# Every second one of the first sixteen weight pieces has its second float32r part subtracted by GpSimd instead of VectorE

## The chip, the cores and the metric

One core of one Trainium2 chip. The metric is the device time in microseconds of one execution; lower is better. The kernel before was timed three times: 563.71, 563.80 and 564.51 us, median 563.8.

## What is computed

Three stages in float32, 2 x 768 = 1536 tokens:

```python
# attention: 2 batches, 8 heads, 768 positions, head size 64
k_sum = k.reshape(B, H, 24, 32, D).max(axis=3)
v_sum = v.reshape(B, H, 24, 32, D).mean(axis=3)
scores_l = where(|i - j| < 16, q @ k.T / 8, -1e9)
scores_s = q @ k_sum.T / 8 + log(32)
a = softmax(concat(scores_l, scores_s));  x = a @ concat(v, v_sum)
# x as 1536 x 512
x = (sigmoid(x @ w_gate) * (x @ w_val)) @ w_out          # hidden size 1536
h = maximum(x @ w1, x @ w2, x @ w3)                      # hidden size 768
out = h @ w_out2
```

## The kernel before

**Two parts for each number.** TensorE multiplies in float32r. So that little of float32 is lost, each operand is held as two parts: a high part, which ScalarE writes by a copy into float32r (`hi`, L348), and the rest, which VectorE subtracts (`lo`, L351). A product is three matmuls: high by high, high by rest, rest by high.

**Weights.** They lie in HBM as 64-bit words (the bits of float64), 48 pieces of 128 x 512. `convert` takes them in the order of use; the pieces of the first block (w_gate, w_val, w_out) are converted a second time for the second batch, so there are 96 conversions. For each one: SP issues a load of 512 KB into `raw` (L398; three buffers), VectorE makes float32 bits of it by three integer instructions into `c` (L405, L410, L414; two buffers), ScalarE writes the high part into `w`, and VectorE the rest (L351, called in `split` at L429). A weight piece may be used when both are there (`wready`); `c` is free when both have read it. The first sixteen, counted from 0, are g0, v0, g1, v1, g2, v2, g3, v3 (gate and value, 128 hidden columns each), o0 to o3 (rows of w_out), g4, v4, g5, v5.

**Attention.** Sixteen units (batch, head pair, half of the sequence), numbered 0 to 15; units 0 to 3 are the first half of batch 0. Per unit: scores (PE L592), their masked maximum (VectorE L599, two times three instructions on `s` in PSUM), exponentials with their sums (ScalarE L605), a reciprocal (L610, L611), the normalisation (VectorE L614 up to unit 5, ScalarE L619 after that), transposes (PE L624), copies (ScalarE L627), the product with the values (PE L634), and the two parts of x (ScalarE L348, VectorE L351 `x<-s,x`). The block maxima of the keys are L516 (`ks`); for batch 1 they are copied into the window's keys (L574, `kw`). The block means of the values are matmuls for batch 0 (L522); for batch 1 GpSimd first adds them up (L527, three additions of 96 partitions with 512, 256 and 128 elements), then one matmul (L532). These additions and the constants are all that GpSimd does.

**First block.** For each half of a batch (`a`) and each group of four hidden pieces: `make_A` computes gate and value (PE L713, 12 matmuls each), ScalarE the sigmoid (L727), VectorE the product (L732, `t`), ScalarE and VectorE the two parts of the hidden piece (L348, L351 `h<-t,h`). Then `make_B` computes the four output blocks of the down projection (PE L747), each of four parts, one per hidden piece, of three matmuls; a block needs all four pieces of `h` and all four `o`. "The first down projection" is that of the first half of batch 0, hidden pieces 0 to 3.

**After that** come the second block (L837, by seven products in place of eight) and the last projection (L944).

**What sets the order.** Every step is a `Task` with an engine, a duration in us that is written in by hand (`add("DVE", 0.602, ...)`), a due time and its dependences. `Plan.order` (L115) goes through them like a clock: each engine takes, of the tasks that can start first, the one that is due first. The result is the order in which the instructions are issued; each engine, SP's DMA queue among them, then executes its own list in that order. A duration or an engine that is changed for one task moves the tasks behind it, on every engine. The planner's durations don't know of one engine slowing another.

Of the kernel before, what the change touches and what calls it, by code (L numbers as in the profile page):

```python
# [9 lines left out]
F32 = mybir.dt.float32  # L10
# [4 lines left out]
ALU = mybir.AluOpType  # L15
# [20 lines left out]
FREE_M = 2  # L36
BY_ACT = 6
BY_DMA = 8
JOINT = 4
SWITCH = 6.0  # L40
SLACK = {"PE": 0.05, "DVE": 0.12, "ACT": 0.1, "POOL": 0.0, "SP": 0.0}
# [31 lines left out]
class Plan:  # L73
# [11 lines left out]
    def add(self, eng, dur, due, fn, deps=(), new=(), uses=(), after=(), tab=None):  # L85
        t = Task(eng, dur, due, fn, [d for d in deps if d], list(new), list(uses), [d for d in after if d], tab)
        self.tasks.append(t)
        return t
# [114 lines left out]
def kernel(  # L203
# [15 lines left out]
    nc = tc.nc  # L219
# [67 lines left out]
    add = plan.add  # L287
# [59 lines left out]
    def hi(dst, src):  # L347
        nc.scalar.activation(out=dst, in_=src, func=ACTF.Copy)  # L348

    def lo(dst, src, h):  # L350
        nc.vector.tensor_tensor(out=dst, in0=src, in1=h.bitcast(F32), op=ALU.subtract)  # L351
# [26 lines left out]
    def first_use(b, nm, f):  # L378
        if nm == "o":
            return due["B", b, (f // GF, 0), 0] + 0.49 * (f % GF)  # L380
        if nm == "l":
            return due["D", 0, 0, 0] + 0.65 * f
        return due[nm, b, f, 0]

    wt, wready = {}, {}

    def convert():
        prev = {}
        n = 0

        def to_float(ck, t):

            nonlocal n
            r = Buf(rp, [128, 2 * 512], I32, "raw", 3)
            c = Buf(cp, [128, 512], I32, "c", 2)

            def load(r=r, ck=ck):
                nc.sync.dma_start(out=r.t, in_=wts[row[ck[1:]]])  # L398

            def half(r, i):  # L400
                return r.t.rearrange("p (f two) -> p f two", two=2)[:, :, i]


            def c1(r=r, c=c):
                nc.vector.tensor_scalar(  # L405
                    out=c.t, in0=half(r, 1), scalar1=5, scalar2=2,
                    op0=ALU.logical_shift_left, op1=ALU.logical_shift_right)

            def c2(r=r, c=c):
                nc.vector.scalar_tensor_tensor(  # L410
                    out=c.t, in0=half(r, 1), scalar=-0x40000000, in1=c.t, op0=ALU.bitwise_and, op1=ALU.bitwise_or)

            def c3(r=r, c=c):
                nc.vector.scalar_tensor_tensor(  # L414
                    out=c.t, in0=half(r, 0), scalar=29, in1=c.t, op0=ALU.logical_shift_right, op1=ALU.bitwise_or)

            n += 1
            l = add("SP", 1.456, t - WLOAD - WLOAD0 * (n <= 10), load, new=[r], after=[prev.get("l")])
            k1 = add("DVE", 0.335, t - 2.7, c1, [l], [c], [r], [prev.get("1")])
            k2 = add("DVE", 0.602, t - 2.3, c2, [k1], [], [c, r])  # L420
            k3 = add("DVE", 0.602, t - 1.6, c3, [k2], [], [c, r])
            prev.update({"l": l, "1": k1})
            return c, k3

        def split(src, view, t, dep, n=512):

            w = Buf(wp, [128, 2, 512], F32R, "w", NW)
            k4 = add("ACT", 0.52 if n == 512 else 0.31, t - 1.0, lambda: hi(w.t[:, 0, 0:n], view()), dep, [w], [src], [prev.get("4")])
            k5 = add("DVE", 0.602 if n == 512 else 0.38, t - 0.5, lambda: lo(w.t[:, 1, 0:n], view(), w.t[:, 0, 0:n]), [k4], [], [src, w])  # L429
            prev["4"] = k4  # L430
            return w, k5

        for ck in chunks:
            t = first_use(*ck) - WREADY
            c, k = to_float(ck, t)
            wt[ck], wready[ck] = split(c, lambda c=c: c.t.bitcast(F32), t, [k])
        for nm, f, b in groups:
            if b == 0:
                blocks(nm, f, to_float, split, prev)
        for ck in last:  # L440
            t = first_use(*ck) - WREADY
            c, k = to_float(ck, t)
            wt[ck], wready[ck] = split(c, lambda c=c: c.t.bitcast(F32), t, [k])
# [106 lines left out]
    def make_unit(u, i):  # L550
# [26 lines left out]
        def vfill(dma):  # L577
            o = vt.t[96:CW].rearrange("p t par h d -> p (t par) (h d)")
            src = vs.t[96:CW, None, :].to_broadcast([NB, 2 * TPU, 2 * D])
            if dma:  # L580
                nc.scalar.dma_start(out=o, in_=src)
            else:
                nc.scalar.activation(out=o, in_=src, func=ACTF.Copy)
# [72 lines left out]
        for h in range(2):  # L656
            m1 = add("DVE", 0.62, T - 9 + h, lambda h=h: maxi(h), [s1, built], [], [ps[h], e[h], nm])
            E.append(add("ACT", 1.14, T - 8 + h, lambda h=h: expo(h), [m1], [], [e[h], nm, sm], tab="E"))
            attention.extend([m1, E[h]])
        joint = i >= JOINT  # L660
        for h in range(2):
# [10 lines left out]
            attention.extend([i1, n1, t1, u1])  # L672
        dma = i >= BY_DMA
        g1 = add("ACT", 0.12 if dma else 0.83, T - 5, lambda: vfill(dma), [kv], [], [vt, vs], [lv])
# [309 lines left out]
    with tc.manual_schedule():  # L984
        idle = const.tile([128, 384], BF16, name="idle")
        nc.vector.memset(idle, 0.0)
        for t in plan.order():
            for b in t.new:
                b.take()
            if t.idle:  # L990
# [3 lines left out]
                n = min(o.shape[1], 384)  # L994
# [62 lines left out]
```

## Time and profile before

| | us |
|---|---|
| median of three runs | 563.8 |
| the profiled execution | 564.15 |
| its span in the trace | 562.2 |
| TensorE busy in the span | 545.4 |
| VectorE busy | 430.6 |
| ScalarE busy | 286.9 |
| GpSimd busy | 16.0 |

The span is the time from the first to the last event that the profile has; some 2 us of the execution lie around it. "Busy" counts the time in which an instruction of the engine runs; matmuls overlap one another, so TensorE can be called busy and yet be behind its pace. In the views in order of time a line stands for one or several instructions of a kind: start, length, engine, line, operation, output and inputs, the count, and in brackets the idle time before it with what ended it. In the chain of waits the second number is the part of the instruction that lies on the chain.

### The profile page before, as it was taken

Reading aid. Unit: us, or ns where it says so; the run is one execution under the profiler, and the core shown is the slowest. Engines: PE = TensorE matmul, PEld = TensorE weight load, DVE = VectorE, ACT = ScalarE, POOL = GpSimd, SP = SyncE. Lnnn points to the kernel's source line nnn. Section 1 sums busy time; section 2 is a strip of 40 time slices with the busy share of each in tenths; the row PEclk is TensorE's granted clock in tenths of the full one; section 3 lists DMA queues with packets and bytes.
Section 4 is the critical chain, followed back from the end, with each engine's and each line's share of the span. In section 5 each row is a group of like instructions: output and inputs, shape, how many; then the busy total and the mean of one; then the engine's idle time right before and its main releaser. Section 6 shows DMA issues by size and latency. Waiting matters only on the chain.

```text
span 562.2 us, 10234 instructions
## 1 busy us (share of the span) xinstructions
PE 545.4 (97%) x3924; PEld 522.4 (93%) x3924; DVE 430.6 (77%) x987; ACT 286.9 (51%) x663; POOL 16.0 (3%) x30
## 2 busy tenths in 40 slices
PE   7799899999999999999999999999999999999997
PEld 7688799998999999999999999999999999997886
DVE  5899949894697598949996996899999997885000
ACT  3789776582765656966441432435344333453111
POOL 2002211000000000000000000000000000000000
PEclk8999999999999999999999999999999999999999
DMA  8999654563265453520652553130322222000111
GB/s 275 311 284 303 192 174 152 154 216 97 85 194 184 145 154 107 170 75 1 188 186 77 157 182 113 53 98 23 105 90 85 77 74 86 28 1 37 57 72 60
DMA packets 24672, 71.96 MB, mean 128 GB/s; under 512 B 3120, under 2 KB 6576, under 8 KB 24624
## 3 DMA queue, kind: packets, MB, share of 16 engines
q1 hardware_dynamic: 21504, 67.58, 38.3%
q10 hardware_dynamic: 3120, 3.74, 1.9%
q8 instruction: 31, 0.51, 0.4%
q14 instruction: 17, 0.14, 0.1%
HBM read 67.57 MB, written 3.15 MB: 126 GB/s over the span
## 4 chain that ended last, share of the span: by engine, by line
PE 79%; DVE 10%; ACT 4%; DMA 4%; issue 1%; SPq 1%; ACTq 0%; DVEq 0%
PE m L713 28%; PE m L747 16%; PE s L837 11%; PE m L837 11%; PE m L944 9%; DVE c L414 2%; DVE c L410 2%; PE s L634 2%; DMA kn<-in_kn_dram 1%; DMA v<-in_vw_dram 1%; DMA vn<-in_vn_dram 1%; DVE w L351 1%; PE s L624 1%; DVE e L599 1%; DVE c L405 1%
## 5 line engine op out<-in xcount | busy, mean ns | idle before, releaser
L713 PE MATMUL m<-x,w 128*128 128x384 f32 x1152 | 211.0, 338 | 0.5 <-ACT t L727 0.3
L713 PEld LDWEIGHTS m<-x,w 128*128 128x128 f32 x1152 | 198.7, 188 | 2.5 <-issue 0.6
L747 PE MATMUL m<-h,w 128*128 128x384 f32 x576 | 107.5, 338 | 0.8 <-DVE h L351 0.7
L747 PEld LDWEIGHTS m<-h,w 128*128 128x128 f32 x576 | 99.2, 188 | 2.4 <-DVE h L351 1.7
L348 ACT ACTIVATE w<-c 128x512 fp32r<-128x512 f32 x96 | 58.1, 610 | 70.4 <-DVE c L414 46.1
L351 DVE TENSOR_TENSOR w<-c,w 128x512 fp32r<-128x512 f32 x96 | 64.4, 671 | 12.6 <-ACT w L348 12.4
L414 DVE SCALAR_TENSOR_TENSOR c<-raw,c 128x512 int32<-128x512 int32 x96 | 66.2, 692 | 0.6
L410 DVE SCALAR_TENSOR_TENSOR c<-raw,c 128x512 int32<-128x512 int32 x96 | 65.7, 686 | 0.6
L837 PE MATMUL m<-x,w 128*128 128x384 f32 x294 | 56.3, 335 | 1.2 <-ACT t L852 1.2
L837 PE MATMUL s<-f,w 128*128 128x384 f32 x294 | 56.0, 334 | 0.0
L837 PEld LDWEIGHTS m<-x,w 128*128 128x128 f32 x294 | 51.3, 188 | 1.6 <-ACT t L852 1.5
L837 PEld LDWEIGHTS s<-f,w 128*128 128x128 f32 x294 | 51.4, 188 | 0.0
L405 DVE TENSOR_SCALAR c<-raw 128x512 int32<-128x512 int32 x96 | 41.0, 430 | 5.1 <-DMA raw<-in_wts_dram 4.1
L727 ACT ACTIVATE t<-m 128x384 f32<-128x384 f32 x48 | 23.4, 491 | 34.9 <-PE m L713 34.6
L732 DVE TENSOR_TENSOR t<-m,t 128x384 f32<-128x384 f32 x48 | 26.6, 554 | 15.0 <-PE m L713 10.5
L348 ACT ACTIVATE h<-t 128x384 fp32r<-128x384 f32 x48 | 25.0, 522 | 25.5 <-DVE t L732 23.6
L605 ACT ACTIVATE e<-e,nm 128x120 f32<-128x120 f32 x96 | 36.6, 383 | 0.2
L351 DVE TENSOR_TENSOR h<-t,h 128x384 fp32r<-128x384 f32 x48 | 27.9, 582 | 5.4 <-ACT h L348 5.4
L954 ACT ACTIVATE c<-m 128x512 f32<-128x512 f32 (+1 forms) x13 | 7.3, 565 | 40.0 <-PE m L944 36.1
L852 ACT ACTIVATE t<-s 128x384 f32<-128x384 f32 x27 | 13.3, 491 | 24.4 <-PE s L837 24.4
L944 PE MATMUL m<-w,x 128*128 128x512 f32 (+1 forms) x126 | 24.9, 359 | 0.0
L944 PE MATMUL m<-w,f 128*128 128x512 f32 x108 | 24.7, 389 | 0.0
(108 smaller groups left out, 588.6 us busy)
## 6 DMA issues: line engine op xcount, KB each, us to landing
raw<-in_wts_dram SPq DMA_DIRECT2D x96, 512.0 KB, 3.6
kn<-in_kn_dram SPq DMA_DIRECT2D x8, 400.0 KB, 7.5
q<-in_qt_dram SPq DMA_DIRECT2D x16, 192.0 KB, 6.4
v<-in_vw_dram SPq DMA_DIRECT2D x16, 192.0 KB, 5.1
kw<-in_kw_dram SPq DMA_DIRECT2D x8, 360.0 KB, 4.1
out_dram<-c ACTq DMA_DIRECT2D x11, 256.0 KB, 2.0
vn<-in_vn_dram SPq DMA_DIRECT2D x8, 256.0 KB, 6.2
v<-in_vw_dram SPq DMA_DIRECT2D x16, 96.0 KB, 4.3
```

The costliest lines, as they stand in the source:

```text
L348: nc.scalar.activation(out=dst, in_=src, func=ACTF.Copy)
L351: nc.vector.tensor_tensor(out=dst, in0=src, in1=h.bitcast(F32), op=ALU.subtract)
L405: nc.vector.tensor_scalar(out=c.t, in0=half(r, 1), scalar1=5, scalar2=2, op0=ALU.logical_shift_left, op1=ALU.logical_shift_right)
L410: nc.vector.scalar_tensor_tensor(out=c.t, in0=half(r, 1), scalar=-0x40000000, in1=c.t, op0=ALU.bitwise_and, op1=ALU.bitwise_or)
L414: nc.vector.scalar_tensor_tensor(out=c.t, in0=half(r, 0), scalar=29, in1=c.t, op0=ALU.logical_shift_right, op1=ALU.bitwise_or)
L605: nc.scalar.activation(out=e[h].t[:, t], in_=e[h].t[:, t], func=ACTF.Exp, scale=-1.0, bias=nm.t[:, h, t:t + 1], accum_out=sm.t[:, h, t:t + 1])
L713: nc.tensor.matmul(ps.t, lhsT=w.t.rearrange("p s (k f) -> p s k f", k=KC)[:, wh, kc], rhs=src[kc // 2].t[:, xh, kc % 2], start=(kc == 0 an ...
L727: k1 = after("t", add("ACT", 0.371, end, lambda: nc.scalar.activation(out=s.t, in_=ps.t, func=ACTF.Sigmoid), [l], [s], [ps], tab="S"))
L732: k2 = after("t", add("DVE", 0.469, end, lambda: nc.vector.tensor_tensor(out=t.t, in0=ps2.t, in1=s.t, op=ALU.mult), [l2, k1], [t], [ps2, s]))
L747: nc.tensor.matmul(ps.t, lhsT=w.t.rearrange("p s (k f) -> p s k f", k=KC)[:, wh, dm], rhs=h.t[:, xh], start=(i == 0 and j == 0), stop=(i = ...
L837: nc.tensor.matmul(ps.t, lhsT=w.t[:, wh, c:c + 128], rhs=x.t[:, xh, kc], start=new and n == 0, stop=n == 5, skip_group_check=True)
L944: nc.tensor.matmul(ps.t[:, c0:c1], lhsT=h.t[:, xh, e, c:c + 128], rhs=w.t[:, wh, c0:c1], start=(f == 0 and i == 0), stop=(f == NF2 - 1 and ...
```

## The change

In `split`, the second part of a piece is subtracted by GpSimd where fewer than sixteen pieces have been made and their number is odd: v0, v1, v2, v3, o1, o3, v4, v5 (pieces 1, 3, 5, 7, 9, 11, 13, 15). The planner takes 1.4 us for it on GpSimd where it took 0.602 us on VectorE. For the other pieces the same subtraction is written out. The lines behind it move by one to five: L351 for weights becomes L433, L348 L349, L405 L406, L410 L411, L414 L415, L351 for x and h L352, L516 L521, L574 L579, L592 L597, L599 L604, L610 L615, L611 L616, L624 L629, L634 L639, L713 L718, L732 L737, L747 L752.

```diff
--- before.py
+++ after.py
@@ -36,6 +36,7 @@
 FREE_M = 2
 BY_ACT = 6
 BY_DMA = 8
+BY_POOL = 16
 JOINT = 4
 SWITCH = 6.0
 SLACK = {"PE": 0.05, "DVE": 0.12, "ACT": 0.1, "POOL": 0.0, "SP": 0.0}
@@ -425,8 +426,12 @@
         def split(src, view, t, dep, n=512):
 
             w = Buf(wp, [128, 2, 512], F32R, "w", NW)
+            pool = len(wready) < BY_POOL and len(wready) % 2 == 1
+            by = (nc.gpsimd if pool else nc.vector).tensor_tensor
+            eng = ("POOL", 1.4) if pool else ("DVE", 0.602 if n == 512 else 0.38)
             k4 = add("ACT", 0.52 if n == 512 else 0.31, t - 1.0, lambda: hi(w.t[:, 0, 0:n], view()), dep, [w], [src], [prev.get("4")])
-            k5 = add("DVE", 0.602 if n == 512 else 0.38, t - 0.5, lambda: lo(w.t[:, 1, 0:n], view(), w.t[:, 0, 0:n]), [k4], [], [src, w])
+            k5 = add(*eng, t - 0.5, lambda: by(out=w.t[:, 1, 0:n], in0=view(), in1=w.t[:, 0, 0:n].bitcast(F32), op=ALU.subtract),
+                     [k4], [], [src, w])
             prev["4"] = k4
             return w, k5
```

Since durations and engines enter the planner, the order changes on all engines up to about a quarter of the program.

On GpSimd, behind the constants, stood the additions of the block means of batch 1 (`vn`, `vr`):

```order
L282 MEMSET masks 64x16
L283 MEMSET masks 64x16
L527 TENSOR_TENSOR vn<-vn 96x2x256
L527 TENSOR_TENSOR vn<-vn 96x2x128
L527 TENSOR_TENSOR vr<-vn 96x128
L527 TENSOR_TENSOR vn<-vn 96x2x256
L527 TENSOR_TENSOR vn<-vn 96x2x128
L527 TENSOR_TENSOR vr<-vn 96x128
```

Now:

```order
L284 MEMSET masks 64x16
L433 TENSOR_TENSOR w<-c,w 128x512 x4
L532 TENSOR_TENSOR vn<-vn 96x2x256
L532 TENSOR_TENSOR vn<-vn 96x2x128
L532 TENSOR_TENSOR vr<-vn 96x128
L433 TENSOR_TENSOR w<-c,w 128x512 x2
L532 TENSOR_TENSOR vn<-vn 96x2x256
L532 TENSOR_TENSOR vn<-vn 96x2x128
L532 TENSOR_TENSOR vr<-vn 96x128
L433 TENSOR_TENSOR w<-c,w 128x512 x2
```

The pieces come in between; each `w` row is a subtraction of one weight piece, and the additions of a later head pair stand ahead of the later pieces.

On VectorE, the stretch between the product of the fourth hidden piece (`t`, L732) and the rest of the third (`h`, L351) before:

```order
L732 TENSOR_TENSOR t<-m,t 128x384
L516 TENSOR_REDUCE ks<-kn 128x24
L405 TENSOR_SCALAR c<-raw 128x512
L574 COPY kw<-ks 128x3x24 x2
L410 SCALAR_TENSOR_TENSOR c<-raw,c 128x512
L351 TENSOR_TENSOR h<-t,h 128x384
```

Now, from the rest of the third hidden piece (`h`) to the product of the fourth (`t`) and one row further (`c` and `raw` are the weight conversion, `sm` the reciprocal of unit 6, `x` that of unit 5):

```order
L352 TENSOR_TENSOR h<-t,h 128x384
L411 SCALAR_TENSOR_TENSOR c<-raw,c 128x512
L615 TENSOR_SCALAR sm<-sm 128x6
L616 RECIPROCAL sm<-sm 128x6
L352 TENSOR_TENSOR x<-s,x 128x384
L415 SCALAR_TENSOR_TENSOR c<-raw,c 128x512
L406 TENSOR_SCALAR c<-raw 128x512
L579 COPY kw<-ks 128x3x24 x2
L737 TENSOR_TENSOR t<-m,t 128x384
L411 SCALAR_TENSOR_TENSOR c<-raw,c 128x512
```

The rest of the third piece stands ahead of the product of the fourth, where it stood behind it, and two more steps of a weight conversion and a reciprocal are between the two.

On TensorE, at the start of the first down projection (`m<-h,w`; three matmuls are one part) with the scores and transposes of units 7 and 6, before:

```order
L713 MATMUL m<-x,w 128x384 x9
L747 MATMUL m<-h,w 128x384 x6
L634 MATMUL s<-at,v 64x64 x12
L592 MATMUL s<-kn,q 64x96 x12
L592 MATMUL s<-ks,q 64x24 x12
L747 MATMUL m<-h,w 128x384 x18
L624 MATMUL s<-ident,e_918 120x128 x3
L747 MATMUL m<-h,w 128x384 x3
L624 MATMUL s<-ident,e_919 120x128 x3
L747 MATMUL m<-h,w 128x384 x9
L634 MATMUL s<-at,v 64x64 x12
```

Now:

```order
L718 MATMUL m<-x,w 128x384 x12
L752 MATMUL m<-h,w 128x384 x6
L597 MATMUL s<-kn,q 64x96 x12
L597 MATMUL s<-ks,q 64x24 x12
L752 MATMUL m<-h,w 128x384 x3
L629 MATMUL s<-ident,e_931 120x128 x3
L752 MATMUL m<-h,w 128x384 x3
L629 MATMUL s<-ident,e_932 120x128 x3
L752 MATMUL m<-h,w 128x384 x15
L639 MATMUL s<-at,v 64x64 x12
L752 MATMUL m<-h,w 128x384 x21
```

Before, 24 matmuls (eight parts) of the projection stood ahead of the first transposes of unit 6; now 9 (three parts) do.

## Rows read from the trace of the kernel before

**Rows 1.** The page, busy times of the engines (share of the span, instructions).

```profile
PE 545.4 (97%) x3924; PEld 522.4 (93%) x3924; DVE 430.6 (77%) x987; ACT 286.9 (51%) x663; POOL 16.0 (3%) x30
```

**Rows 2.** Busy time by stretch: TensorE, weight loads, VectorE, ScalarE, GpSimd, clock, DMA share, GB/s.

```profile
30.00:70.00 40.00, 36.72 (x489) 32.60 (x481) 39.75 (x129) 35.29 (x99) 5.48 (x6) 1.00 0.83 262
```

**Rows 3.** The chain of waits, 24 to 110 us: start, us on the chain, what.

```profile
29.40 0.56 DVE x L351
...
32.27 0.20 DVE e L599
...
33.28 0.60 DVE w L351
...
40.66 0.60 DVE c L410
41.27 0.34 DVE c L405
...
63.73 0.86 DVE ks L516
...
64.92 0.23 DVE kw L574 x2
...
65.74 0.48 DVE h L351
```

**Rows 4.** TensorE in order of time, 59 to 69 us: start, us, what, idle before.

```profile
59.45 0.52 PE L624 MATMUL s<-ident,e 128*120 128x128 f32 x3 [1.58 <-DVE e L614]
...
66.27 2.18 PE L747 MATMUL m<-h,w 128*128 128x384 f32 x11 [0.45 <-DVE h L351]
```

**Rows 5.** Groups on GpSimd, 76 to 79 us: busy us, mean ns, idle before.

```profile
L527 POOL TENSOR_TENSOR vn<-vn 96x512 f32<-96x512 f32 x1 | 1.3, 1278 | 5.8 <-DMA vn<-in_vn_dram 5.8
```

**Rows 6.** VectorE and then GpSimd in order of time, near GpSimd's bursts.

```profile
30.92 0.42 DVE L405 TENSOR_SCALAR c<-raw 128x512 int32<-128x512 int32 x1
...
43.92 0.69 DVE L351 TENSOR_TENSOR w<-c,w 128x512 fp32r<-128x512 f32 x1
...
48.02 0.55 DVE L351 TENSOR_TENSOR h<-t,h 128x384 fp32r<-128x384 f32 x1
...
53.41 1.56 DVE L351 TENSOR_TENSOR w<-c,w 128x512 fp32r<-128x512 f32 x1
55.01 0.84 DVE L405 TENSOR_SCALAR c<-raw 128x512 int32<-128x512 int32 x1
...
67.47 1.45 DVE L351 TENSOR_TENSOR h<-t,h 128x384 fp32r<-128x384 f32 x1
68.85 0.27 DVE L599 CUSTOM_DVE_ANT_0 e<-s,masks 128x120 f32<-128x120 f32 x1
...
97.68 1.48 DVE L414 SCALAR_TENSOR_TENSOR c<-raw,c 128x512 int32<-128x512 int32 x1
...
53.14 2.42 POOL L527 TENSOR_TENSOR vn<-vn 96x512 f32<-96x512 f32 x2 [48.11 <-PE s L592]
...
67.23 2.29 POOL L527 TENSOR_TENSOR vn<-vn 96x512 f32<-96x512 f32 x2 [11.06 <-DMA vn<-in_vn_dram]
...
97.33 2.43 POOL L527 TENSOR_TENSOR vn<-vn 96x512 f32<-96x512 f32 x2
```

**Rows 7.** The chain of waits of the whole span: start, us, what.

```profile
251.91 16.64 PE m L713 x96
```

**Rows 8.** TensorE in order of time, 98 to 129 us.

```profile
98.48 1.47 PE L747 MATMUL m<-h,w 128*128 128x384 f32 x7
100.23 0.62 PE L747 MATMUL m<-h,w 128*128 128x384 f32 x2 [0.29 <-DVE h L351]
...
100.94 2.33 PE L747 MATMUL m<-h,w 128*128 128x384 f32 x12
103.42 0.92 PE L634 MATMUL s<-at,v 120*64 120x64 f32 x24
...
128.29 0.92 PE L634 MATMUL s<-at,v 120*64 120x64 f32 x24 [1.04 <-issue]
```

## The prediction

> **What bounds the kernel now.** The page first [rows 1]: TensorE is busy for 545.4 of 562.2 us, VectorE (DVE) for 430.6, GpSimd (POOL) for 16.0. By that share VectorE is not the bound, and relieving it would be worth nothing. A share is an average, though, so the next view is the table of stretches [rows 2]: between 30 and 70 us VectorE is busy for 39.75 of 40 us and GpSimd for 5.48, and TensorE has the holes. The chain of waits agrees [rows 3]: from the second L351 into x at 29.40 to the third L351 into h, which ends at 66.22, it runs through VectorE nearly without a break, and the pieces between are the weight conversion (L405, L410, L414, L351), the attention and the hidden parts. At 66.27 TensorE takes the chain over. In the list of TensorE's work [rows 4] one sees the holes: 1.58 us at 59.45 for a normalised e, 0.45 at 66.27 for the third h. So the change can act on the time in one place: how early VectorE gets through its work up to about 68.9 us, where the fourth h is done and TensorE's first down projection (L747) can go on.
>
> **What is taken off VectorE.** One subtraction into w takes 0.60 us of VectorE's time [rows 3] (the L351 w at 33.28). Eight leave it, so 8 x 0.60 = 4.8 us by about 95 us. What matters is the part ahead of the fourth h. By the order, between the second x and the fourth h VectorE had nine subtractions into w and now has four: 5 x 0.60 = 3.0 us less. The planner fills that room with work that stood behind the fourth h: one more conversion (L405, L410, L414), one more key maximum (L516), two copies into kw (L574), three score maxima (L599). From the chain [rows 3] that is 0.34 + 0.60 + 0.60 (L414 as L410) + 0.86 + 0.23 + 3 x 0.20 = 3.23 us. So VectorE has **0.23 us more to do before the fourth h**, not less. The third h has gained (in the order it now stands ahead of the fourth t), yet all four hidden pieces are needed before the first bank of the down projection is complete, and TensorE executes in order.
>
> **What it costs on GpSimd.** The page shows no 128x512 subtraction there. The nearest row is the L527 addition of 96x512, the same 512 elements on each partition: 1278 ns [rows 5]. I take 1.28 us. As a duration this is covered: the pieces are wanted later than they are ready. The first bank needs o1 and o3 (pieces 9 and 11) at about 60 and 69 us. On GpSimd they stand behind the first L527 burst, whose two larger additions ended at 53.14 + 2.42 = 55.56 [rows 6] and a short third one some 0.6 later; 56.2 + 1.28 = 57.5. If that cover goes, the third rival below gives the price.
>
> **What it costs VectorE.** This is the unknown price. Before the change GpSimd ran next to a busy VectorE only in a few bursts, and they can be read one by one [rows 6]. When L527 starts at 53.14, the L351 into w takes 1.56 us in place of its 0.69 (+0.87). At 67.23 the L351 into h takes 1.45 in place of 0.55 (+0.90). At 97.33 an L414, as large as the L351 of 0.69, takes 1.48 (+0.79). The smaller L527 behind the first stretches an L405 from 0.42 to 0.84. The L599s that run beside the second burst keep their 0.27. So an instruction of VectorE that reads two tensors from SBUF, or an L405, waits almost until GpSimd's addition is done; one that reads PSUM does not. Bounds of the stall for one moved subtraction: nothing (it meets only L599s, or an idle VectorE, as before the x at 29.40), and 0.90 us. Between the second x and the fourth h the sensitive kinds make some 60% of VectorE's time, they come in runs, and all three large bursts with work beside them met one. I take 0.65 us, three quarters of the middle of those three. That is more than the 0.60 that moving the subtraction saves: **on balance the move gives VectorE nothing**.
>
> The rows give the stall to the kinds that read two tensors. The Trainium skill, in "Advanced Engine Details and Errata" (VectorE Performance Modes), says that the second port shared with GpSimd makes GpSimd and two-port-mode Vector instructions block each other; by that alone only the L405s would suffer. "GPSIMD Engine Reference" (Key points) of the Trainium skill adds instructions with two SBUF inputs. The trace agrees with the second. By the first the stall would be nearly nothing, which is the first rival's sum.
>
> **The sum.** Pieces 3, 5, 7, 9 and 11 run on GpSimd between the second x and the fourth h (piece 1 falls where VectorE waits anyway before 29.40). The fourth h started at 67.47. With the change: 67.47 + 0.23 + 5 x 0.65 = 70.95. Its own length is 0.55, or 1.45 if the second L527 burst meets it again as in [rows 6]; half of that 0.90 gives an end near 71.95, against 68.92. TensorE goes on 3.0 us later. By then it has done one L747 part less than before (three matmuls at 0.173, the pace of 16.64 us for 96 [rows 7]: 0.52) and three transposes more (about 0.3), which leaves 0.2 more to do: **+3.2 us**. From there TensorE is the bound, with the same work as before, and a delay stays unless it swallows a later wait. The list shows two [rows 8]. Seven L747s at 98.48 take 1.75 us to the next, 1.21 at pace, and twelve at 100.94 take 2.48 to the L634 at 103.42, 2.08 at pace: they wait for an h, 0.94 in all. A TensorE that comes 3 us later finds that h ready, because VectorE then has 4.8 us less of its own work; I take back 0.8. The wait of 1.04 at 128.29 is named issue, no engine's lateness: nothing back. Sum +3.2 - 0.8 = **+2.4 us**.
>
> Edits that I cost at nothing: two more table loads on ScalarE at about 60 us (1.28 us each). They stand ahead of the scaling of unit 6, which waits for VectorE's reciprocal at least as long by the same sum; were they exposed, up to 1.3 us. Weight loads move one or two places ahead on SP's queue, past q and v loads; the DMA engines are at 0.83 of their time there and move 262 GB/s [rows 2], so a load that is passed lands later by about 512 KB at that rate, 2 us, and I see no TensorE wait for q or v in that stretch that would grow by it.
>
> The profiled execution took 564.15 us, 0.35 above the median of 563.8. 564.15 + 2.4 = 566.55; against the median **566.2 us**.
>
> **Rivals.**
> First, the other side: the stalls don't come about, because the pieces fall beside L599, L732 and L516 or because only L405 is hit. Then the fourth h ends at 67.47 + 0.23 + 0.55 = 68.25, 0.65 earlier than before, less 0.2 for the changed order, and the 0.8 at 99 us comes back too: 563.8 - 1.25 = **562.5 us**. For it: more than half of VectorE's instructions by number are the short L599s, which keep their length. Against: three bursts of three. It decides when the mean stall of a piece is under about 0.05 us. By the narrower note of the Trainium skill, above, it would go this way.
> Second, half the stall, 0.33 us a piece: 5 x 0.33 + 0.23 + 0.2 - 0.8, plus the half chance of the second burst, less what h already lost to it (0.45 - 0.90): +0.8, **564.6 us**. Within 0.2%, which is 1.1 us and about what a measurement of this kernel can tell from no change.
> Third, worse: GpSimd's queue. Pieces 9 and 11 stand behind an L527 that waits for a vn load. If that load lands 4 us later than before (53.1), piece 9 is ready at 61.5 or later and the first L747s wait for it, and all five stalls come in full: 5 x 0.9 + 0.23 + 0.45 + 0.2 = 5.4, without the 0.8 back: **569.1 us**. Against it: the place of that load on SP's queue is unchanged.
>
> **Chances.** Forecast (slower by more than 1.1 us, near 566.2) 0.54; third rival 0.08; second 0.22; first 0.16. So slower 0.62, same 0.22, faster 0.16. The range, 562.4 to 568.8, takes in the first rival and, at the top, the forecast with all five stalls at 0.90 (+1.25), the second burst met in full (+0.45) and 0.8 not given back: 568.7. What is left out is the third rival and a part of the first. For the forecast alone it is 565.0 to 568.7.
>
> **What would show it.** L351 into w (now L433 on GpSimd) at 1.2 to 1.4 us; some L410, L414 or L351 at about 1.5 us beside nearly every one of them; VectorE still above 39 of 40 us from 30 to 70; the fourth h ending at 71 to 73 us and TensorE waiting for an h there; after 130 us the same list of TensorE's work, 2 to 3 us later. I am wrong if VectorE's instructions keep their lengths beside GpSimd's, if the fourth h comes before 69 us, or if TensorE's wait at that place is for something else.

## The result and the profile after

The changed kernel takes **568.03 us** (median of four runs, 567.61 to 568.19), the kernel before in the same comparison 563.95: a ratio of 1.0071 with a 95% interval of 1.0053 to 1.0089. Run again beside other kernels later it gave 568.27, ratio 1.0087 (1.0060 to 1.0115). So it is slower by some 4 us, as forecast in sign, and by more than the 2.4 us of the sum. The profiled execution took 567.93 us with a span of 566.0.

The page's busy line answers to [rows 1], then the table of stretches to [rows 2]:

```profile
PE 546.3 (97%) x3924; PEld 524.7 (93%) x3924; DVE 427.3 (75%) x979; ACT 290.9 (51%) x665; POOL 26.4 (5%) x38
```

```profile
30.00:70.00 40.00, 35.78 (x438) 32.23 (x435) 38.12 (x127) 35.86 (x94) 11.12 (x10) 0.91 0.78 251
```

Three things are new between 30 and 70 us: GpSimd is busy for 11.12 us (5.48 before), VectorE is no longer without a gap (38.12 of 40, 39.75 before), and the granted clock is 0.91 where it was 1.00. Next the group of the eight moved subtractions, on GpSimd:

```profile
L433 POOL TENSOR_TENSOR w<-c,w 128x512 fp32r<-128x512 f32 x8 | 10.7, 1333 | 65.9 <-ACT w L349 65.9
```

VectorE in order of time, the instructions between the second x and the fourth h that took longer than their kind, or waited, and the fourth h itself:

```profile
33.53 0.17 DVE L615 TENSOR_SCALAR sm<-sm 128x3 f32<-128x3 f32 x1 [0.52 <-ACT e L610]
...
37.59 1.42 DVE L406 TENSOR_SCALAR c<-raw 128x512 int32<-128x512 int32 x1
...
47.99 0.79 DVE L352 TENSOR_TENSOR h<-t,h 128x384 fp32r<-128x384 f32 x1
...
51.91 0.56 DVE L737 TENSOR_TENSOR t<-m,t 128x384 f32<-128x384 f32 x1 [0.98 <-PE m L718]
52.38 0.94 DVE L415 SCALAR_TENSOR_TENSOR c<-raw,c 128x512 int32<-128x512 int32 x1
53.25 0.70 DVE L615 TENSOR_SCALAR sm<-sm 128x6 f32<-128x6 f32 x1
...
54.52 1.55 DVE L619 TENSOR_TENSOR e<-e,sm 128x360 f32<-128x360 f32 x1
...
64.40 0.78 DVE L352 TENSOR_TENSOR h<-t,h 128x384 fp32r<-128x384 f32 x1
...
70.66 0.94 DVE L352 TENSOR_TENSOR h<-t,h 128x384 fp32r<-128x384 f32 x1
```

GpSimd in order of time, over the same stretch and up to 97 us:

```profile
30.54 1.47 POOL L433 TENSOR_TENSOR w<-c,w 128x512 fp32r<-128x512 f32 x1 [17.40 <-ACT w L349]
37.44 1.29 POOL L433 TENSOR_TENSOR w<-c,w 128x512 fp32r<-128x512 f32 x1 [5.43 <-ACT w L349]
46.93 1.43 POOL L433 TENSOR_TENSOR w<-c,w 128x512 fp32r<-128x512 f32 x1 [8.21 <-ACT w L349]
51.48 2.44 POOL L532 TENSOR_TENSOR vn<-vn 96x512 f32<-96x512 f32 x2 [3.12 <-DMA vn<-in_vn_dram]
54.00 0.46 POOL L532 TENSOR_TENSOR vr<-vn 96x128 f32<-96x128 f32 x1
54.41 1.27 POOL L433 TENSOR_TENSOR w<-c,w 128x512 fp32r<-128x512 f32 x1
63.42 1.35 POOL L433 TENSOR_TENSOR w<-c,w 128x512 fp32r<-128x512 f32 x1 [7.74 <-ACT w L349]
...
93.53 1.29 POOL L433 TENSOR_TENSOR w<-c,w 128x512 fp32r<-128x512 f32 x1 [4.89 <-ACT w L349]
94.78 2.16 POOL L532 TENSOR_TENSOR vn<-vn 96x512 f32<-96x512 f32 x2
```

Put side by side, the two lists give the price of each piece. Piece 3 (30.54) ran beside score maxima and stretched nothing; piece 5 (37.44) made an L406 1.42 for 0.42; piece 7 (46.93) an h 0.79 for 0.55; piece 9 (54.41) the normalised e of unit 5 1.55 for 0.52; piece 11 (63.42) an h 0.78 for 0.55. That is 0 + 1.00 + 0.24 + 1.03 + 0.23 = 2.50 us.

The size follows from the place. Piece 5 ends at 37.44 + 1.29 = 38.73, and the L406 that started at 37.59 ends 0.28 us later, at 39.01; the e ends 0.39 behind piece 9, the two h 0.42 and 0.41 behind pieces 7 and 11. Each is 0.13 or 0.14 short of the instruction's own length. So a stalled instruction behaves as if it began 0.13 us before GpSimd's ends, and its stall is what is left of GpSimd's instruction at its start, less 0.13. An instruction that started first keeps its length: beside the start of piece 7 an L406 (46.79) took 0.42. There it is GpSimd that waits: piece 7 took 1.43 and piece 3, which started 0.31 us before the end of an L411, 1.47, where piece 5 took 1.29.

TensorE in order of time shows what it became there, and at about 99 us and 131 us the places of [rows 8]:

```profile
36.83 0.54 PE L629 MATMUL s<-ident,e 128*120 128x128 f32 x3 [0.76 <-DVE x L352]
...
43.16 0.62 PE L718 MATMUL m<-x,w 128*128 128x384 f32 x2 [0.66 <-DVE x L352]
...
56.22 0.52 PE L629 MATMUL s<-ident,e 128*120 128x128 f32 x3 [1.16 <-DVE e L619]
...
57.72 0.77 PE L629 MATMUL s<-ident,e 128*120 128x128 f32 x3 [0.51 <-DVE e L619]
...
99.56 0.62 PE L752 MATMUL m<-h,w 128*128 128x384 f32 x2 [1.13 <-DVE h L352]
...
131.48 0.92 PE L639 MATMUL s<-at,v 120*64 120x64 f32 x24 [0.86 <-issue]
```

The start differs from execution to execution (the second x comes at 28.77 to 32.30 us), so the table that the experiments are read with counts from the start of the second x on VectorE (29.40 before, 28.79 after), in us, one profiled execution each. The third column is the block of 51 gate and value matmuls at about 80 us, the fourth the L634 that is the last row of [rows 8] (L639 after).

| kernel | order, who subtracts | fourth h ends | 51 matmuls start | last row |
|---|---|---|---|---|
| before | old, VectorE | 39.52 | 50.32 | 98.89 |
| after | new, GpSimd | 42.81 | 53.62 | 102.69 |
| after, again | new, GpSimd | 43.90 | 54.66 | 103.55 |
| order only | new, VectorE | 43.33 | 53.81 | 102.27 |
| fill, new order | new, GpSimd fills | 41.14 | 51.75 | 99.49 |
| old order | old, GpSimd | 39.37 | 51.26 | 101.58 |
| fill, old order | old, GpSimd fills | 38.58 | 50.12 | 98.61 |
| idle subtractions | old, VectorE | 40.18 | 52.49 | 101.15 |
| after, with empty matmuls | new, GpSimd | 43.32 | 53.78 | 102.61 |
| before, with empty matmuls | old, VectorE | 39.17 | 49.84 | 97.80 |
| twelve pieces | new, GpSimd | 43.44 | 54.29 | 102.29 |
| all but piece 9 | old, GpSimd | 38.17 | 50.00 | 100.25 |
| all but 9, fill | old, GpSimd fills | 38.25 | 49.03 | 97.11 |
| pieces 1, 3, 11 | old, GpSimd | 37.74 | 49.30 | 97.63 |

### The profile page after: what moved, and what is told of

It is laid out like the page before. It is cut to its first block, busy times and chain, and to the rows that moved or that the text cites. A ratio compares the mean times of both kernels' runs of the same rounds, so it can differ in the third digit from the quotient of the medians.

```text
span 566.0 us, 10244 instructions
## 1 busy us (share of the span) xinstructions
PE 546.3 (97%) x3924; PEld 524.7 (93%) x3924; DVE 427.3 (75%) x979; ACT 290.9 (51%) x665; POOL 26.4 (5%) x38
## 4 chain that ended last, share of the span: by engine, by line
PE 83%; DVE 6%; ACT 4%; DMA 4%; issue 1%; SPq 1%; ACTq 0%; DVEq 0%
PE m L718 31%; PE m L752 17%; PE s L842 11%; PE m L842 11%; PE m L949 9%; PE s L639 2%; DMA q<-in_qt_dram 1%; PE s L629 1%; DVE c L415 1%; DMA raw<-in_wts_dram 1%; DMA vn<-in_vn_dram 1%; DVE c L411 1%; ACT e L610 1%; DVE c L406 1%; PE s L597 1%
## 5 line engine op out<-in xcount | busy, mean ns | idle before, releaser
L718 PE MATMUL m<-x,w 128*128 128x384 f32 x1152 | 213.1, 340 | 1.9 <-ACT x L349 1.0
L718 PEld LDWEIGHTS m<-x,w 128*128 128x128 f32 x1152 | 201.4, 190 | 3.8 <-ACT x L349 1.1
L752 PE MATMUL m<-h,w 128*128 128x384 f32 x576 | 107.0, 338 | 1.1 <-DVE h L352 1.1
L752 PEld LDWEIGHTS m<-h,w 128*128 128x128 f32 x576 | 99.3, 188 | 2.1 <-DVE h L352 1.5
L349 ACT ACTIVATE w<-c 128x512 fp32r<-128x512 f32 x96 | 58.1, 611 | 66.3 <-DVE c L415 42.9
L433 DVE TENSOR_TENSOR w<-c,w 128x512 fp32r<-128x512 f32 x88 | 57.8, 658 | 13.6 <-ACT w L349 13.3
L411 DVE SCALAR_TENSOR_TENSOR c<-raw,c 128x512 int32<-128x512 int32 x96 | 65.9, 688 | 0.6
L415 DVE SCALAR_TENSOR_TENSOR c<-raw,c 128x512 int32<-128x512 int32 x96 | 65.8, 688 | 0.6
L842 PEld LDWEIGHTS m<-x,w 128*128 128x128 f32 x294 | 51.3, 188 | 1.6 <-ACT t L857 1.5
L406 DVE TENSOR_SCALAR c<-raw 128x512 int32<-128x512 int32 x96 | 42.8, 449 | 5.0 <-DMA raw<-in_wts_dram 4.0
L732 ACT ACTIVATE t<-m 128x384 f32<-128x384 f32 x48 | 23.5, 492 | 36.3 <-PE m L718 36.0
L737 DVE TENSOR_TENSOR t<-m,t 128x384 f32<-128x384 f32 x48 | 26.6, 555 | 16.3 <-PE m L718 11.9
L349 ACT ACTIVATE h<-t 128x384 fp32r<-128x384 f32 x48 | 25.0, 523 | 25.7 <-DVE t L737 23.8
L610 ACT ACTIVATE e<-e,nm 128x120 f32<-128x120 f32 x96 | 36.8, 386 | 0.8 <-DVE nm L604 0.5
L352 DVE TENSOR_TENSOR h<-t,h 128x384 fp32r<-128x384 f32 x48 | 27.6, 576 | 6.4 <-ACT h L349 6.3
```

Of the source, the lines that this page charges most:

```text
L406: nc.vector.tensor_scalar(out=c.t, in0=half(r, 1), scalar1=5, scalar2=2, op0=ALU.logical_shift_left, op1=ALU.logical_shift_right)
L411: nc.vector.scalar_tensor_tensor(out=c.t, in0=half(r, 1), scalar=-0x40000000, in1=c.t, op0=ALU.bitwise_and, op1=ALU.bitwise_or)
L415: nc.vector.scalar_tensor_tensor(out=c.t, in0=half(r, 0), scalar=29, in1=c.t, op0=ALU.logical_shift_right, op1=ALU.bitwise_or)
L433: k5 = add(*eng, t - 0.5, lambda: by(out=w.t[:, 1, 0:n], in0=view(), in1=w.t[:, 0, 0:n].bitcast(F32), op=ALU.subtract), [k4], [], [src, w])
L610: nc.scalar.activation(out=e[h].t[:, t], in_=e[h].t[:, t], func=ACTF.Exp, scale=-1.0, bias=nm.t[:, h, t:t + 1], accum_out=sm.t[:, h, t:t + 1])
L718: nc.tensor.matmul(ps.t, lhsT=w.t.rearrange("p s (k f) -> p s k f", k=KC)[:, wh, kc], rhs=src[kc // 2].t[:, xh, kc % 2], start=(kc == 0 an ...
```

## The experiments

**The change taken apart.** Five runs: the new order alone, GpSimd alone, the relief with hardly any contention (in either order), contention without relief. "Contention" is one engine slowing the other. The lines that a run adds move its line numbers by up to ten; operation and tiles show what is meant.

New order, VectorE executes all pieces:

```diff
-            by = (nc.gpsimd if pool else nc.vector).tensor_tensor
+            by = nc.vector.tensor_tensor
```

> The changed kernel's order on every engine, but VectorE executes the eight subtractions, at the place where the planner had put GpSimd's. No contention, and 8 x 0.6 us more on VectorE. Contention theory (a GpSimd subtraction costs VectorE about what it saves): the two nearly cancel, 566 to 568.5 us, VectorE's lengths all normal, the subtraction of unit 5's normalisation at 0.5 in place of 1.55 us. Order theory (the new order alone costs the 4 us, whoever subtracts): 567.5 to 569. If GpSimd's pieces cost VectorE far more than 0.6 us each: below 566.

Measured: 566.95 us, ratio 1.0058 (1.0043 to 1.0073). TensorE in order of time:

```profile
54.92 0.52 PE L629 MATMUL s<-ident,e 128*120 128x128 f32 x3 [1.74 <-DVE e L619]
...
57.02 0.87 PE L629 MATMUL s<-ident,e 128*120 128x128 f32 x3 [1.11 <-DVE e L619]
...
99.59 0.62 PE L752 MATMUL m<-h,w 128*128 128x384 f32 x2 [0.75 <-DVE h L352]
```

With nothing moved to GpSimd the new order costs 1.0058 x 563.6 - 563.6 = 3.3 us: the planner's room is filled with other work, and VectorE, which in truth has no room, comes to the fourth h 3.8 us later.

GpSimd subtracts, in the old order (the planner still books the time on VectorE):

```diff
+            pool = len(wready) < BY_POOL and len(wready) % 2 == 1
+            by = (nc.gpsimd if pool else nc.vector).tensor_tensor
+            eng = ("DVE", 0.602 if n == 512 else 0.38)
```

> The order of the kernel before on every engine, but GpSimd executes the eight subtractions where VectorE did. Contention theory: VectorE saves 0.6 and loses about 0.65 to 0.9 us a piece, 563.5 to 565.5 us, no faster than before. Order theory: the old order is kept, so the saving of up to 3 us ahead of the fourth h shows: 561 to 563.

Measured: 566.5 us, ratio 1.0066 (1.0044 to 1.0089), slower than either theory had it. The fourth h is not later than before (39.37), so the lateness of the fourth h in the changed kernel belongs to the order. TensorE is late all the same. VectorE, then GpSimd, then TensorE in order of time:

```profile
56.88 1.40 DVE L406 TENSOR_SCALAR c<-raw 128x512 int32<-128x512 int32 x1
58.31 1.12 DVE L411 SCALAR_TENSOR_TENSOR c<-raw,c 128x512 int32<-128x512 int32 x1
61.01 0.43 DVE L406 TENSOR_SCALAR c<-raw 128x512 int32<-128x512 int32 x1 [1.58 <-POOL w L433]
```

```profile
56.46 2.41 POOL L532 TENSOR_TENSOR vn<-vn 96x512 f32<-96x512 f32 x2 [5.36 <-PE s L629]
58.96 0.79 POOL L532 TENSOR_TENSOR vr<-vn 96x128 f32<-96x128 f32 x1
59.71 1.27 POOL L433 TENSOR_TENSOR w<-c,w 128x512 fp32r<-128x512 f32 x1
```

```profile
63.23 0.52 PE L629 MATMUL s<-ident,e 128*120 128x128 f32 x3 [2.62 <-DVE e L619]
```

Piece 9 stands in GpSimd's queue behind three vn additions. Until it is subtracted its `c` is not free, there are only two, and VectorE's next conversion waits 1.58 us with the normalised e of unit 5 behind it (the expectation of a later run calls it unit 6; VectorE normalises units 0 to 5 only, two instructions each, and this is the twelfth). Before that the vn additions themselves stretched an L406 and an L411 by 1.4 (three instructions by 1.55 in the kernel before).

The relief with hardly any contention: GpSimd writes zeros instead, and subtracts eight columns only (the low parts of eight pieces are missing). First in the new order, then in the old:

```diff
+            if pool:
+                def by(out, in0, in1, op):
+                    nc.gpsimd.memset(out.bitcast(F32), 0.0)
+                    nc.gpsimd.tensor_tensor(out=out[:, 0:8], in0=in0[:, 0:8], in1=in1[:, 0:8], op=op)
```

> The changed kernel with its order, but on GpSimd the eight subtractions are left out: it fills the 512 columns with zeros and subtracts only the first 8 columns, so that all waits stay; the low part of these eight weight pieces is missing from the products. Contention theory: a fill does not hold VectorE back, the lengths are normal, TensorE's clock stays at full speed from 30 to 70 us, and the time falls to 562.5 to 564.5 us. Order theory: still 567 to 568.5.

Measured: 564.65 us, ratio 1.0020 (1.0000 to 1.0041), with no wait for an h at about 99 us. The clock was 0.96 from 30 to 70 us and not at full speed as expected. The run isn't free of stalls: the first vn additions and the fill behind them lengthen an e, a subtraction into w and an L406 by 1.8 us together. TensorE's longest wait there, 1.64 us for the transposes at 55.87, ended with ScalarE's `v`, which ran behind a table load of 1.28 and ended 0.11 us after VectorE's e.

> The order of the kernel before; GpSimd fills the low part of the eight pieces with zeros and subtracts only 8 columns (the low part of these pieces is missing from the products), so VectorE is relieved of eight subtractions and is not held back. Contention theory: relief alone is worth 1 to 2 us, 561.5 to 563 us, against 566.5 for the same order with real subtractions. If relief is worth nothing in this order: 563.5 to 564.5.

Measured: 563.54 us, ratio 0.9997 (0.9975 to 1.0020). The relief of all eight, in the old order, gains nothing that can be measured. Here too a `c` waits for piece 9 behind the vn additions:

```profile
57.16 0.71 DVE L406 TENSOR_SCALAR c<-raw 128x512 int32<-128x512 int32 x1 [1.10 <-POOL w L436]
```

The contention without the relief: the kernel before, with a useless subtraction of 128x360 on GpSimd behind each of the eight pieces.

```diff
+                if pool:
+                    m = masks.rearrange("p a c -> p (a c)")
+                    nc.gpsimd.tensor_tensor(out=idle[:, 0:360], in0=m, in1=m, op=ALU.subtract)
```

> The kernel before, order and work unchanged, but behind each of the eight subtractions GpSimd makes one useless subtraction of 128 x 360 (the masks from themselves, written to the idle tile as zeros). Contention alone, without relief. Contention theory: each stalls VectorE by some 0.5 us, five or six of them in the stretch where VectorE bounds, so 566 to 568 us, with TensorE's clock lower somewhere between 40 and 65 us if waits are what lowers it. Order theory: 563.7 to 564.5, nothing.

Measured: 566.59 us, ratio 1.0069 (1.0048 to 1.0089). Nothing waits for these subtractions, VectorE has all its work in the old order, and it is about as slow as the changed kernel. But they wait for no piece either, so they don't lie where the pieces do: one ran at 12.21, three in a row at 23.10, where an L406 took 1.00, and two at 73.56. The second x comes at 30.51 for 29.40. So the run shows that GpSimd's work alone can cost as much, and not that the eight pieces cost this by contention. The other two, 1.98 us together, lie right behind the first vn burst at 58.07, and VectorE reads there:

```profile
55.25 1.40 DVE L406 TENSOR_SCALAR c<-raw 128x512 int32<-128x512 int32 x1
56.57 1.22 DVE L434 TENSOR_TENSOR w<-c,w 128x512 fp32r<-128x512 f32 x1
57.71 1.69 DVE L411 SCALAR_TENSOR_TENSOR c<-raw,c 128x512 int32<-128x512 int32 x1
59.32 1.00 DVE L406 TENSOR_SCALAR c<-raw 128x512 int32<-128x512 int32 x1
```

```profile
62.12 0.52 PE L634 MATMUL s<-ident,e 128*120 128x128 f32 x3 [3.12 <-DVE e L624]
```

Its L411 is 1.0 us over its 0.68, its second L406 0.6 over its 0.42; TensorE's wait for the normalised e grew from the 1.58 of [rows 4] to 3.12. From the second x on, 2.2 us are lost by the 51 matmuls.

What follows: with a fill in place of the subtraction the change costs 1.1 us; the real subtraction adds 2.9 to 3.8 (1.0071 and 1.0087 less 1.0020, of 563.6; each ratio is known to some 1 us). That is contention and, since a subtraction takes GpSimd 1.3 us and the fill with its eight columns 0.7, what waits behind it. The order alone costs 3.3, of which the relief gives 2.1 back. Two more table loads on ScalarE (24 for 22) belong to the new order; no run separates them from it.

**The half clock.** After the change the granted clock is 0.57 in 44 to 48 us and 0.59 in 58 to 62 (means; the lower of its two levels is 0.50). TensorE had been busy for 2.33 of 4 us in the stretch before each. That waiting by itself lowers the clock isn't shown: in the second execution of the changed kernel TensorE was busy for 2.34 of 4 us from 40 to 44 and the clock stayed at 1.00 in 44 to 48, and in the run with the idle subtractions it stayed at 1.00 behind the longest wait of all, 3.12 us, so that the sign named in that run's expectation is missing. The rows of 58 to 62 us, after the change and then with the idle subtractions (TensorE first, clock third from the end):

```profile
58.00:62.00 4.00, 4.00 (x17) 4.00 (x16) 4.00 (x14) 2.97 (x7) 0.00 (x0) 0.59 0.53 191
```

```profile
58.00:62.00 4.00, 1.00 (x6) 0.68 (x4) 4.00 (x6) 0.63 (x1) 1.96 (x3) 1.00 0.13 50
```

To see whether this half clock costs time, empty matmuls were put into the holes, of the changed kernel and of the kernel before:

```diff
+FILL = {(3, 1): 3, (5, 's'): 6, (5, 0): 6, (5, 1): 4}
...
+            fillers[s0] = FILL.get((i, "s"), 0)
...
+            fillers[t1] = FILL.get((i, h), 0)
...
+            t.idle += fillers.get(t, 0)
```

> The changed kernel with 19 empty bf16 matmuls more, of the kind that the program already uses in its first 25 us, ahead of four steps at which TensorE waited (3 before the last transposes of unit 3, 6 before the scores of unit 5, 6 and 4 before its transposes); some 3 us of matmuls in all. Clock theory (a TensorE that waits falls to half clock and the half clock costs some of the 4 us): granted clock from 30 to 70 us near 1.00 in place of 0.91, and 565.5 to 567 us. If the half clock is only where TensorE would wait anyway: 568 to 570, the empty matmuls being extra work.

> The kernel before with the same 19 empty matmuls: the control of the filling. Its clock is at full speed from 30 to 70 us without them, so clock theory expects no gain from them there: 563.5 to 566 us, by how many of them find TensorE waiting.

Measured: 568.74 us, ratio 1.0090 (1.0061 to 1.0119), and 563.98, ratio 1.0006 (0.9983 to 1.0028). In the first the table of stretches has the clock at 1.00 again, and TensorE, now in time, waits for the fourth h:

```profile
30.00:70.00 40.00, 36.62 (x490) 31.69 (x482) 39.12 (x115) 36.51 (x96) 11.06 (x10) 1.00 0.76 248
```

```profile
72.70 1.14 PE L756 MATMUL m<-h,w 128*128 128x384 f32 x5 [1.17 <-DVE h L354]
```

No cost of the half clock can be seen, to within the 0.3% of the interval: what it takes, the fourth h would take. In the changed kernel TensorE came to that place later, when the fourth h was done (71.60), so no wait for it is seen there.

**The queue at 95 us.** The wait at 99.56 grew to 1.13 us, from the 0.29 of [rows 8]. The third pair of vn additions ran at 76.26 before, alone; now it is held behind pieces 13 and 15 and meets VectorE at 94.78. GpSimd before, then VectorE after the change, where two L406 take 2.31 for 0.76:

```profile
76.26 2.09 POOL L527 TENSOR_TENSOR vn<-vn 96x512 f32<-96x512 f32 x2 [5.80 <-DMA vn<-in_vn_dram]
```

```profile
94.92 2.31 DVE L406 TENSOR_SCALAR c<-raw 128x512 int32<-128x512 int32 x2
```

With these two pieces on VectorE (the edit is to the changed kernel, and the planner, which reads it too, makes another order behind the twelfth piece):

```diff
-BY_POOL = 16
+BY_POOL = 12
```

> The change for the first twelve pieces only (six on GpSimd in place of eight). Queue theory: pieces 13 and 15 held the third block-mean addition back on GpSimd from about 77 to 95 us, where it met a busy VectorE and made TensorE wait 1.1 us at 99.6; without them it runs at about 77 us again, that wait is 0.5 us or less, and the time is 0.5 to 1 us below the change: 566.8 to 567.6. If those two pieces play no part: 568.

Measured: 568.95 us, ratio 1.0079 (1.0052 to 1.0107): no gain. Yet in the trace the third pair is early again and the wait is short, GpSimd and then TensorE:

```profile
80.79 2.10 POOL L532 TENSOR_TENSOR vn<-vn 96x512 f32<-96x512 f32 x2 [7.04 <-DMA vn<-in_vn_dram]
```

```profile
106.28 0.62 PE L752 MATMUL m<-h,w 128*128 128x384 f32 x2 [0.29 <-DVE h L352]
```

From the 51 matmuls to the last row it takes 48.00 us, where the changed kernel takes 49.07 and 48.89. So this term is about 1 us, and it is under what these runs scatter by (566.19 to 569.74). Nor is the queue shown to be all of the wait. In the run with the new order alone the third pair ran at 77.95, nothing was held, and TensorE still waited 0.75 there, with the subtractions of pieces 13 and 15 on VectorE.

**Which pieces pay.** The waits for `c` pointed to piece 9. All but that one, in the old order, with the fill and with the real subtraction (edits to the two runs in the old order above), and the changed kernel beside them:

```diff
-            pool = len(wready) < BY_POOL and len(wready) % 2 == 1
+            pool = len(wready) < BY_POOL and len(wready) % 2 == 1 and len(wready) != 9
```

> The old order, seven of the eight pieces (all but piece 9) given to GpSimd as a fill with zeros and eight columns of the subtraction; the low part of these pieces is missing. In the run with all eight, piece 9 stood in GpSimd's queue behind a burst of the vn additions, its c came free late (VectorE waited 1.10 us for it) and TensorE's wait for the normalised e of unit 6 grew from 1.58 to 2.37 us. Theory 'relief was eaten by the queue': without piece 9 that wait falls to 1.6 us or less, the span from the second x to the block of 51 gate and value matmuls is 49.3 us or less (50.3 before) and the time is 0.8 to 2 us under before. Theory 'VectorE is no bound that pays': the wait shrinks and something else is late instead, the time stays within 0.5 us of before.

> The old order, seven pieces (all but piece 9) really subtracted by GpSimd. Theory 'contention costs what a piece saves or more': 1 to 3 us over before, with long L406, L411, L352 beside the pieces; theory 'queue wait of piece 9 was most of the 3 us of the run with all eight': within 1 us of before, or faster. This is the one real version that could beat the kernel before.

> The changed kernel itself, beside the two others on the same chip. All theories: 1.0053 to 1.0089 of before, as measured. In the trace: the fourth h ends 42.5 to 43.5 us behind the start of the second x (39.5 before), the 51 gate and value matmuls start some 53.6 behind it.

Measured: 561.83 us, ratio 0.9970 (0.9947 to 0.9993); 564.79, ratio 1.0018 (0.9992 to 1.0045); 568.27, ratio 1.0087 as given above, with the fourth h at 43.90 instead of 42.5 to 43.5 and the 51 matmuls at 54.66 instead of 53.6. The relief of VectorE does pay, 1.7 us (0.4 to 3.0 by the interval), once piece 9 is left where it was; that speaks against the theory that VectorE is no bound that pays. TensorE's wait for the e, though, is 1.78 there and not 1.6 or less. And without piece 9 the real subtraction costs 1.0 us, which its interval no longer tells from nothing, instead of 3.7 (1.0066). Which of its pieces cost is read from VectorE in order of time, in the run with the real subtraction:

```profile
39.01 1.43 DVE L411 SCALAR_TENSOR_TENSOR c<-raw,c 128x512 int32<-128x512 int32 x1
...
46.62 1.33 DVE L352 TENSOR_TENSOR h<-t,h 128x384 fp32r<-128x384 f32 x1
...
91.79 1.51 DVE L406 TENSOR_SCALAR c<-raw 128x512 int32<-128x512 int32 x1
93.34 1.11 DVE L411 SCALAR_TENSOR_TENSOR c<-raw,c 128x512 int32<-128x512 int32 x1
```

Pieces 5 and 7 (GpSimd at 38.62 and 46.26) stretch one instruction each by 0.75 and 0.78, more than the 0.60 that they save; at 91.28 the third vn pair comes right behind piece 15 and stretches an L406 and an L411 by 1.5 in all. From the 51 matmuls to the last row it takes 50.25 us there, before 48.57. Pieces 3 and 11 (31.40 and 60.31) stretch nothing. So the last run leaves GpSimd these two, and piece 1, which runs ahead of the second x (an edit to the run with the real subtraction in the old order):

```diff
+            pool = len(wready) in (1, 3, 11)
```

> The old order; GpSimd really subtracts only pieces 1, 3 and 11, those of the run without piece 9 beside which VectorE had only score maxima and no instruction was stretched. Pieces 5 and 7 (each stretched an instruction by some 0.75 us for the 0.60 saved) and 13 and 15 (the third pair of vn additions stood behind them and met VectorE at 91 us, where before it ran at 76) are on VectorE. Theory 'only the place of the piece counts': 1 to 2 us under before, no instruction over 1.0 us beside the three pieces, third vn burst back at 76 to 79 us. Theory 'each subtraction on GpSimd costs what it saves': within 1 us of before.

Measured: **562.02 us** (561.11 to 564.27, 12 runs) against 563.88: ratio 0.9971 (0.9955 to 0.9988). It beats both kernels. The third vn pair, expected at 76 to 79 us, is early again. GpSimd and then VectorE beside its piece 11:

```profile
60.21 1.49 POOL L433 TENSOR_TENSOR w<-c,w 128x512 fp32r<-128x512 f32 x1 [3.88 <-ACT w L349]
...
74.72 2.08 POOL L532 TENSOR_TENSOR vn<-vn 96x512 f32<-96x512 f32 x2 [4.83 <-DMA vn<-in_vn_dram]
```

```profile
60.66 0.27 DVE L604 CUSTOM_DVE_ANT_0 e<-s,masks 128x120 f32<-128x120 f32 x1
...
61.07 0.55 DVE L737 TENSOR_TENSOR t<-m,t 128x384 f32<-128x384 f32 x1
```

During the whole subtraction VectorE does score maxima and a product from PSUM, at their usual length. Three subtractions of 0.60 are 1.8 us of relief at most; 1.6 are gained (0.0029 x 563.9; 0.7 to 2.5 by the interval). Which of the three gains it was not taken apart.

## Why the prediction was right, and where it was not

- **"In one place: how early VectorE gets through its work up to about 68.9 us": right about VectorE, too narrow about the place.** In nine of the fourteen rows of the table, before and after among them, the 51 matmuls start 10.5 to 10.9 us behind the end of the fourth h. The two move together; a wait of TensorE for that very h is listed only after the change with the empty matmuls. The other five (11.5 to 12.3) are runs in the old order with more work on GpSimd, where TensorE was held earlier, by the normalised e of unit 5. With GpSimd in the old order the fourth h is on time and the kernel is 3.7 us slower.
- **"0.23 us more to do before the fourth h, not less": right, and the heart of it.** The order alone, with no relief, delays the fourth h by 3.8 us (3.23 of other work by the sum), the old order with GpSimd by nothing.
- **1.28 us on GpSimd: right** (1333 ns on average, 0.05 over, [rows 5]).
- **0.65 us of stall for each piece: a little high.** 2.50 / 5 = 0.50, within the bounds of 0 and 0.90 but for two pieces that cost 1.00 and 1.03. The kinds were right: two inputs in SBUF, or an L406; those that read PSUM keep their length. The note in "Advanced Engine Details and Errata" of the Trainium skill (VectorE Performance Modes) names only two-port-mode instructions and would have given nothing for h and e. "GPSIMD Engine Reference" of the Trainium skill (Key points) names two SBUF inputs as well, and the trace agrees: e 1.55 for 0.52. What the prediction had no term for is where in GpSimd's instruction the other starts: 0.24 and 0.23 for pieces 7 and 11, late in it, 1.00 and 1.03 for pieces 5 and 9, early in it.
- **The start of the fourth h: right by misses that cancel, which is luck.** Forecast 67.47 - 29.40 + 0.23 + 3.25 = 41.55 from the second x, measured 70.66 - 28.79 = 41.87. The stalls were 0.75 less, and the first vn burst stretched VectorE by 0.80 us where it had been 1.55; against that VectorE stood idle for 1.88 us from 30 to 70 where it was 0.25 before, 0.98 of it for TensorE at 51.91. That a VectorE that is late makes TensorE late, and then waits for it, was missing from the sum. It bears on the first rival too: with the fill the new order still costs 1.1 us, where that rival had a gain of 1.25, and VectorE is idle for 1.13 of these 40 us.
- **"TensorE goes on 3.0 us later ... +3.2": the size right, the sign to look for wrong.** The 51 matmuls start 3.30 later. But no wait for an h stands at 72 us: TensorE had waited earlier, for x and e, and then ran at half clock. With the clock held up the forecast wait is there, 1.17 us, and no gain in time is seen.
- **"I take back 0.8": the step that failed.** I reasoned that h at 99 us would be ready because VectorE has 4.8 us less of its own work. But VectorE waits for TensorE shortly before, for 1.78 and 1.44 us, in both kernels (at 82.69 and 85.30 before, 85.39 and 87.99 after), so that what it was relieved of earlier is lost; only the work behind these waits counts. There I did not price what stands in GpSimd's queue behind pieces 13 and 15, though the order of GpSimd's list was in view. The wait grew to 1.13 instead, and the last row is 3.80 later instead of 2.4. How much of it is the queue and how much the order stays open (0.75 by the order alone). Another 0.6 us of the span lies behind that row; it is scatter, for in the second execution the stretch behind it is as long as before (433.95 and 433.91 us).
- **The third rival had the right queue, in the wrong kernel and with another consequence.** Piece 9 behind a vn burst does not bind in the new order. In the old order it takes most of the loss (1.0066 with it, 1.0018 without; the two were compared on different occasions and their intervals just touch), by the `c` that it holds and not, as the rival had it, by matmuls that wait for the piece. The rival's sum is also 0.9 too high: it leaves out the 0.90 that the h had already lost before, which the second rival takes off. So it comes to about 568.2, inside the range that was to leave it out.

## What to carry to other kernels

Work that goes to a slower engine is paid for three times: by instructions of the other engine that stall beside it, by what stands behind it in its new queue (and by the buffers that it holds until then), and by a planner that fills the room it believes to be free. So look at each moved instruction by itself: here three of eight together, in the old order, were worth moving (0.9971), and all eight cost 0.7%. Its stall is what is left of the moved instruction when the other engine's next sensitive instruction starts, so what stands beside it decides. A planner that prices neither stalls nor held buffers should have the execution changed first and the order left alone, so that the two effects can be measured apart.

## What the runs showed of the hardware

- Beside a GpSimd subtraction of two SBUF tensors that is already running, VectorE's instructions with two SBUF inputs, and the one-input L406, take until 0.13 us before its end and then their own length: 0.42 became 1.42, 0.52 became 1.55, 0.55 became 1.33. One that is running when GpSimd's starts keeps its length, and GpSimd's is longer (1.47 and 1.43 for 1.29). Beside the vn additions even a 128x6 TENSOR_SCALAR took 0.70 for 0.16. Score maxima and products that read PSUM keep their 0.27 and 0.55, and so does the key maximum L521 (0.95 beside pieces 7 and 11), which reads one tensor from SBUF.
- With a GpSimd fill of 128x512 with zeros (0.52 us) and a subtraction of eight columns in place of the whole one, the change cost 1.1 us in place of 4.0.
- The granted clock fell to 0.57 and 0.59 behind stretches in which TensorE was busy for 2.33 of 4 us, and held at 1.00 behind one of 2.34 and within one of 1.00. No cost in time was seen, with another engine's lateness to cover it.
